# A list-scheduled attention and MLP-mixer kernel on one Trainium2 core: another cost model, order of loads and way of spreading constants

## The chip, the cores and the metric

The kernel runs on one core of one Trainium2 chip. The core has a matrix engine (TensorE, PE in the profile), a vector engine (VectorE, DVE), a scalar engine (ScalarE, ACT), a general engine (GpSimd, POOL), and queues that issue DMAs between the chip's memory and the on-chip buffer SBUF. TensorE writes to PSUM, from which VectorE and ScalarE read. Each engine works through its own instructions in program order and waits at each for the data that it needs.

The metric is the time of one execution on the device in microseconds. The kernel before took 294.46 us, the median of three runs (293.62 to 296.24).

## The reference

Four batches of 768 tokens, 8 heads of 64 (so 512 columns): attention in which each token sees the first 4 tokens and the 128 up to itself, then a residual MLP block with a mixing over tokens and one over channels.

```python
# q, k, v: (4, 8, 768, 64); n_sink = 4, window = 128
scores = q @ k.transpose(0, 1, 3, 2) / sqrt(64)
rel = pos[:, None] - pos[None, :]
keep = (pos[None, :] < n_sink) | ((rel >= 0) & (rel < window))
a = softmax(where(keep, scores, -1e9))
x = (a @ v).transpose(0, 2, 1, 3).reshape(4, 768, 512)

tok = einsum('ts,bsd->btd', w_tok, alpha1 * x + beta1)   # w_tok: 768 x 768
u = x + lam * tok
ch = maximum((alpha2 * u + beta2) @ w_ch1, 0) @ w_ch2    # 512 x 2048, 2048 x 512
out = u + lam * ch
```

All inputs and the output are fp32.

## The kernel before

**The plan.** The body does not issue instructions directly. It adds about a thousand tasks to a `Plan`, each with a priority, the engines that could run it and an estimated cost on each, the tasks it comes after, and the buffers it uses. `Plan.emit` then does list scheduling: it always takes the task that can start earliest by its own clock (ties by priority, then by the earlier end) and emits its instructions on that engine. So the estimated costs, the estimated landing time of a load (`lands`, with all loads on one modelled channel) and the priorities set the order on every engine's queue. The estimates set nothing else: on the chip each instruction waits only for its data and for its buffer. Buffers have a fixed number of homes (`homes`); a task whose buffer kind has no free home is passed over.

**The work.** For batch b:

- `load_qk` (L290) loads 8 pieces of `q` and `k` of 384 KB into `nat` (8 homes); `load_v` (L297) loads 6 pieces of `v` of 256 KB into `vnat` (4 homes). Batch 0's `v` comes as 12 pieces of 128 KB (`load_v0`, L306), six of them in a buffer that occupies one home of `wst`.
- `trans` (L352) casts a `nat` piece to fp16 (`n16`), transposes it on TensorE (`tp`) and copies it to `qkT`. For later batches the cast is GpSimd's and the copy VectorE's.
- `sinks`, `fill_vs`, `scores` and `pv` do the attention: products `S` on TensorE, `E` = exp on ScalarE, the mask on VectorE (for batch 0 the mask is added by TensorE instead), then `pv`, and `x` = `pv` times a reciprocal on VectorE. The scaled `xh` follows, on GpSimd for later batches (`tmp`, then `xh`).
- `tok` (L600) is the mixing over tokens: six accumulating matmuls for each of six token tiles, each needing all six `xh`. The add to `x` follows on VectorE, then the cast `u` on ScalarE.
- `uTs` transposes `u`, and VectorE applies alpha2 and beta2. `mlp1` (`h`, then relu to `hT`) and `mlp2` (`ch`) are the channel MLP; the add of `ch` and the store follow.

On TensorE the attention of batch b+1 is placed between the MLP's matmuls of batch b.

**The weights** are loaded once, in batch 0. `w_tok` comes in 6 pieces, is cast by ScalarE with a running sum (`rs`, the row sums), and is transposed on TensorE to `wtokT`. `w_ch1` and `w_ch2` come in 4 pieces of 1 MB each through `wst` (2 homes); `cast_w1` (L578) makes `w1f`, and `cast_w2` (L586) makes `w2f`, the weights times `lam`. The vectors `lam`, `alpha1` and `beta1` are loaded as broadcasts to all 128 partitions (`load_const`, 256 KB each), and GpSimd makes `la1_b` = alpha1 * lam and `lb1_b` = beta1 * lam.

**The order of loads.** All loads but those of alpha2 and beta2 go through one queue (SP), in the order of the plan. For batch 0: half of `q` and `k`, two `v` pieces, `lam`, `alpha1`, four `v` pieces, the other half of `q` and `k`, six `v` pieces, three of `w_tok`, the first of `w_ch1`, `beta1`, three of `w_tok`, then the other weights. The loads of batch b+1 have priority `w0` (b = 0) or `w0 - 30`, and no predecessor but a free home, so SP also takes them whenever a weight load finds no home.

Of the kernel before, what the change touches and what calls it, by code (L numbers as in the profile page):

```python
# [29 lines left out]
class Task:  # L30
    def __init__(self, prio, engs, fn, after, uses, mode, lands):
        self.prio, self.engs, self.fn, self.uses = prio, engs, fn, uses
        self.mode, self.lands = mode, lands
        self.needs = [a for a in after if a is not None and a.seen is None]
        self.ready = max([0.0] + [a.seen for a in after if a is not None and a.seen is not None])
        self.then = []
        self.seen = None


class Plan:  # L40
# [8 lines left out]
    def add(self, prio, engs, fn, after=(), uses=(), mode=None, lands=0.0):  # L49
        t = Task(prio, engs, fn, after, uses, mode, lands)  # L50
        for b in uses:
            b.left += 1
        for a in t.needs:
            a.then.append(t)
        self.tasks.append(t)
        return t

    def emit(self):
# [13 lines left out]
        channel = 0.0  # L72
        done = 0
        while done < len(self.tasks):
            best = None
            for r, t in open_:
# [57 lines left out]
def kernel(  # L134
# [56 lines left out]
        "wst": (sb, [P, 4, 512], FP32),  # L191
# [5 lines left out]
        "rec": 2, "u16": 4, "uT": 1, "hT": 2, "wst": 2, "d": 4, "S": 2,  # L197
# [14 lines left out]
    alpha2_c = const.tile([P, NC], FP32, name="alpha2_c")  # L212
    beta2_c = const.tile([P, NC], FP32, name="beta2_c")
    rs = const.tile([P, NR], FP32, name="rs")
    nc.scalar.dma_start(alpha2_c, moe_alpha2.rearrange("(c p) -> p c", p=P))
    nc.scalar.dma_start(beta2_c, moe_beta2.rearrange("(c p) -> p c", p=P))
# [6 lines left out]
    )  # L223
    mask0 = const.tile([P, 1, 2 * P], FP16, name="mask0")
# [36 lines left out]
    )  # L261
    bias0 = const.tile([P, 1, 2 * P], FP16, name="bias0")
# [27 lines left out]
    def load_qk(p, b, hp, t):  # L290
# [4 lines left out]
            uses=[bf], lands=1030)  # L295

    def load_v(p, b, r):  # L297
# [4 lines left out]
            uses=[bf], lands=950)  # L302
# [3 lines left out]
    def load_v0(p, G, r):  # L306
        if r == 0:
            v0[G] = Buf(("uT", "wst")[G], [P, NR, 4, D], FP32, f"v0_{G}")
        bf = v0[G]
        done["v0", G, r] = add(  # L310
            p, {SP: 520}, lambda e: nc.sync.dma_start(  # L311
                bf.t[:, r], v[0, 4 * G : 4 * G + 4, r * P : (r + 1) * P, :].rearrange("h p d -> p h d")),
            uses=[bf], lands=470)
# [3 lines left out]
    def load_wtok(p, ti):  # L317
        if ti % 3 == 0:
# [5 lines left out]
            uses=[bf], lands=1000)  # L324
# [3 lines left out]
    def load_w(p, key, src):  # L328
        bf = wst[key] = Buf("wst", None, None, f"wst_{key}")
        done["wst", key] = add(  # L330
            p, {SP: 400}, lambda e: nc.sync.dma_start(bf.t, src), uses=[bf], lands=2600)

    def load_w1(p, i):
        load_w(p, f"w1_{i}", moe_w_ch1[:, i * 512 : (i + 1) * 512].rearrange("(c p) f -> p c f", p=P))

    def load_w2(p, i):
        load_w(p, f"w2_{i}", moe_w_ch2[i * 512 : (i + 1) * 512, :].rearrange("(a p) d -> p a d", p=P))

    def load_const(p, name, tile_, src):
        done[name] = add(  # L340
            p, {SP: 500}, lambda e: nc.sync.dma_start(tile_, src.unsqueeze(0).to_broadcast([P, DM])),
            lands=800)
# [7 lines left out]
    ANY = {DVE: 555, ACT: 835, POOL: 859}  # L350

    def trans(p, b, hp, t, engs, evac, cast_p=None):  # L352
# [20 lines left out]
        a = add(p - 2 if cast_p is None else cast_p, engs, cast, [done["nat", b, hp, t]], [src, n16])  # L373
        a = add(p, {PE: 330}, tr, [a], [n16, pt])
# [5 lines left out]
    def sinks(p, b, Gs=(0, 1)):  # L380
# [24 lines left out]
        a = add(p, {DVE: 360 if n == 1 else 600}, ksf, qk + [done.get(("sk", b - 1, 0))], [o])  # L405
        a = add(p + 0.1, {PE: 240}, mm, [a], [o, pt], mode="col")
        done["sk", b, Gs[0]] = a
        done["es", b, Gs[0]] = add(p + 0.2, {ACT: 595}, ex, [a], [pt, es[b]])

    def fill_vs(p, b):  # L410
        pt = Buf("d", [P, H, D], FP32, f"vsp{b}")

        def mm(e):
            nc.tensor.matmul(pt.t, sel, vf[0][:, :, 0:D], start=True, stop=True)

        def ev(e):
            nc.vector.tensor_mul(vs[:, :, 0:D], pt.t, bmf.to_broadcast([P, H, D]))

        vfs = [done["vf", b, 0]] if b else [done["vf", 0, 0, 0], done["vf", 0, 0, 1]]
        a = add(p, {PE: 215}, mm, vfs, [pt])  # L420
        done["vsmm", b] = a
        prior = [done.get(("pv", b - 1, r, G)) for r in range(NR) for G in range(2)]
        done["vs", b] = add(p + 0.1, {DVE: 690}, ev, [a] + prior, [pt])

    def scores(p, b, j, Gs, bias=False):
# [29 lines left out]
        cost = sum(n * w * 0.42 + (2 * n * w * 0.42 + 100 if bias else 0) for _, _, n, _, _ in units)  # L455
        a = add(p, {PE: cost}, mm, qk, [o] + [u[3] for u in units], mode="row")
        for G, hps, n, pS, eT in units:
# [8 lines left out]
            if not bias:  # L466
# [5 lines left out]
                x_ = add(p + 0.2, {DVE: 60 + 2 * n * w * 0.72}, mk, [x_], [eT])  # L472
# [5 lines left out]
    def pv(p, b, r, G):  # L478
# [25 lines left out]
        if r >= 2:  # L504
            after += [done["vs", b], done["es", b, G if b == 0 else 0]]
            uses.append(es[b])
        a = add(p, {PE: 128 + 250}, mm, after, uses)
# [14 lines left out]
        if b == 0:  # L522
# [6 lines left out]
            done["xh", b, r, G] = add(p + 8.2, {POOL: 730, DVE: 420}, half, [a, done["la1"]], [bx, bh])  # L529
# [20 lines left out]
    def cast_v0(p, G, r):  # L550
        bf = v0[G]
        done["vf", 0, r, G] = add(
            p, {POOL: 400, DVE: 230, ACT: 400},
            lambda e: copy(e, vf[r][:, 4 * G : 4 * G + 4, 0:D], bf.t[:, r]), [done["v0", G, r]], [bf])


    def cast_wtok(p, ti):
# [3 lines left out]

        def cast(e):
            nc.scalar.activation(
                w.t.rearrange("p r i -> p (r i)"), src.t[:, ti % 3, :], AF.Copy,
                accum_out=rs[:, ti : ti + 1])

        def tr(e):
# [6 lines left out]
        done["wtokT", ti] = add(  # L574
            p + 0.2, {DVE: 560, ACT: 810}, lambda e: copy(e, wtokT[:, :, ti * P : (ti + 1) * P], pt.t),
            [a], [pt])

    def cast_w1(p, i):  # L578
        src = wst[f"w1_{i}"]
        for c in range(NC):  # L580
            done["w1", i, c] = add(
                p, {ACT: 600, POOL: 645, DVE: 330},
                lambda e, c=c: copy(e, w1f[:, c, i * 512 : (i + 1) * 512], src.t[:, c, :]),
                [done["wst", f"w1_{i}"]], [src])

    def cast_w2(p, i):  # L586
        src = wst[f"w2_{i}"]
        for a in range(4):
            done["w2", 4 * i + a] = add(
                p, {DVE: 900, POOL: 1400},  # L590
                lambda e, a=a: engine[e].tensor_mul(w2f[:, 4 * i + a, :], src.t[:, a, :], lam_b),  # L591
                [done["wst", f"w2_{i}"], done["lam"]], [src])
# [7 lines left out]
    def tok(p, b, ti):  # L600
# [5 lines left out]
        def mm(e):  # L606
            for si in range(NR):
                nc.tensor.matmul(  # L608
                    pt.t, wtokT[:, si, ti * P : (ti + 1) * P], hs[si].t,
                    start=(si == 0), stop=(si == NR - 1))  # L610
# [10 lines left out]
        def uc(e):  # L621
            copy(e, bu.t, bx.t.rearrange("p h d -> p (h d)"))

        after = [done["wtokT", ti]] + [
            done["xh", b, r, G] for r in range(NR) for G in ((0, 1) if b == 0 else (1,))]
        a = done["tok", b, ti] = add(p, {PE: 6 * 214}, mm, after, [pt] + hs)
        before = [done["xh", b, ti, G] for G in ((0, 1) if b == 0 else (1,))]
        if b == 0:
            before.append(add(p - 0.5, {DVE: 870}, res,
                              before + [done["rs", ti], done["lb1"], done["x", b, ti, 0], done["x", b, ti, 1]],  # L630
                              [bx]))
        a = done["u", b, ti] = add(p + 0.1, {DVE: 690}, ua, [a] + before, [pt, bx])
        done["u16", b, ti] = add(p + 0.2, {ACT: 620}, uc, [a], [bx, bu])

    def uTs(p, b, chk, cp):
# [14 lines left out]
        for ci in range(2):  # L650
            c = 2 * cp + ci

            def ev(e, ci=ci, c=c):
                nc.vector.tensor_scalar(  # L654
                    out=bo.t[:, c, chk * NTOK : (chk + 1) * NTOK], in0=pt.t[:, ci, :],
                    scalar1=alpha2_c[:, c : c + 1], scalar2=beta2_c[:, c : c + 1],
                    op0=ALU.mult, op1=ALU.add)

            done["uT", b, chk, c] = add(p + 0.1 + 0.01 * ci, {DVE: 470}, ev, [a], [pt, bo])
# [62 lines left out]
    for r in range(2):  # L722
        load_v0(at(), 0, r)
    load_const(at(), "lam", lam_b, moe_lam)
    load_const(at(), "a1", la1_b, moe_alpha1)
    for r in range(2, NR):
# [5 lines left out]
    for ti in range(3):  # L732
        load_wtok(at(), ti)
    load_w1(at(), 0)
    load_const(at(), "b1", lb1_b, moe_beta1)
    for ti in range(3, NR):
        load_wtok(at(), ti)
    for i in range(1, 4):
        load_w1(at(), i)
    for i in range(4):  # L740
        load_w2(at(), i)

    done["la1"] = add(-890, {POOL: 1270}, lambda e: nc.gpsimd.tensor_mul(la1_b, la1_b, lam_b),
                      [done["lam"], done["a1"]])
    done["lb1"] = add(-790, {POOL: 1270}, lambda e: nc.gpsimd.tensor_mul(lb1_b, lb1_b, lam_b),
                      [done["lam"], done["b1"]])
    for i, (hp, t) in enumerate(QK_ORDER):
        g = -950 + 5 * i if i < 4 else -890 + 8 * (i - 4)
        trans(g, 0, hp, t, ANY, {DVE: 955, ACT: 880}, cast_p=g - 20)
# [3 lines left out]
    fill_vs(-890, 0)  # L753
# [14 lines left out]
    for b in range(B):  # L768
# [10 lines left out]
        else:  # L779
            seq = [("tok", ti) for ti in range(5)] + [("uT", 0, 0), ("uT", 0, 1), ("tok", 5)]  # L780
# [80 lines left out]
```

## Time and profile before

| | us |
|---|---|
| median of three runs | 294.46 (293.62 to 296.24) |
| the profiled execution | 292.78 |
| its span in the trace | 291.1 |
| TensorE busy in the span | 264.5 |
| VectorE busy | 177.5 |
| ScalarE busy | 116.2 |
| GpSimd busy | 117.6 |
| moved by DMA | 37.01 MB |

The profile is a trace of one execution. A span of 40 slices shows which engine is busy when, a digit for each slice in tenths. Rows of the timeline give start, duration, engine, line and operation, and in brackets how long the engine had been idle before it and who ended that. Rows of a wait give who waited for whom, the total, the number of times and the longest. Names with the number left out stand for all tiles of the name, and `L591` is line 591 of the kernel.

### The profile page before, as it was taken

To read this page: it belongs to the slowest core of one execution; us is meant where nothing else is said; L and a number is where in the kernel's file an instruction comes from. 1 tells how busy PE (TensorE), PEld (TensorE's weight loads), DVE (VectorE), ACT (ScalarE), POOL (GpSimd) and SP (SyncE) were. 2 spreads that over 40 slices of the span, in tenths; PEclk is the share of its full clock that TensorE was granted. 3 is DMA by queue.
4 is the path that set the end of the run, shared out by engine and by line. 5 is a ranking of instruction groups with operands and counts; after the bars stand their busy time and mean duration, and the time that the engine had idled before them with its cause. 6 is when DMAs were issued, how large, how long until landed. Compare 5 with 4: busy or idle time off the path is not lost.

```text
span 291.1 us, 4977 instructions
## 1 busy us (share of the span) xinstructions
PE 264.5 (91%) x1984; PEld 144.8 (50%) x1984; DVE 177.5 (61%) x338; ACT 116.2 (40%) x189; POOL 117.6 (40%) x127
## 2 busy tenths in 40 slices
PE   1789599889594999999999999999999999999994
PEld 0344366555352454565654545665654545665441
DVE  4576998575999744896645417977654336543111
ACT  2489555458361001258772003367741014442000
POOL 4365896361699883340465632202435500000000
PEclk9999789999799899999999999999999999999999
DMA  6999999999970365510021111000001110000111
GB/s 206 295 299 368 386 321 275 373 252 339 309 269 0 108 181 145 155 65 0 2 65 46 72 43 67 0 2 0 3 1 74 72 71 3 0 0 2 72 72 72
DMA packets 43814, 37.01 MB, mean 127 GB/s; under 512 B 27280, under 2 KB 35472, under 8 KB 43792
## 3 DMA queue, kind: packets, MB, share of 16 engines
q1 hardware_dynamic: 42736, 36.71, 40.2%
q8 instruction: 15, 0.25, 0.4%
q10 hardware_dynamic: 1056, 0.00, 0.2%
q14 instruction: 7, 0.06, 0.1%
HBM read 30.41 MB, written 6.29 MB: 126 GB/s over the span
## 4 chain that ended last, share of the span: by engine, by line
PE 66%; DMA 15%; DVE 11%; SPq 4%; issue 1%; POOL 1%; ACT 0%; ACTq 0%; DVEq 0%; POOLq 0%
PE ch L693 27%; PE h L669 25%; DMA wst_w<-in_moe_w_ch_dram 8%; PE tok L608 6%; DMA nat<-in_q_dram 4%; DVE w2f L591 4%; SPq L311 3%; PE pv L493 2%; DVE E L470 2%; PE S L448 2%; DMA beta_c<-in_moe_beta_dram 2%; SPq L294 1%; DMA v<-in_v_dram 1%; PE tp L367 1%; DVE qkT L206 1%; DVE uT L654 1%
## 5 line engine op out<-in xcount | busy, mean ns | idle before, releaser
L669 PE MATMUL h<-uT,w1f 128*128 128x384 f16 x512 | 92.9, 329 | 4.4 <-DVE x L517 3.0
L693 PE MATMUL ch<-w2f,hT 128*128 128x512 f16 x384 | 90.1, 384 | 3.7 <-DVE x L517 3.2
L669 PEld LDWEIGHTS <-w1f 128*128 128x128 f16 x512 | 47.8, 98 | 36.5 <-issue 8.0
L693 PEld LDWEIGHTS <-hT 128*128 128x128 f16 x384 | 36.1, 99 | 45.2 <-DVE x L517 3.7
L675 ACT ACTIVATE hT<-h 128x384 f16<-128x384 f32 x87 | 42.4, 493 | 37.4 <-PE h L669 37.1
L204 ACT CAST u<-x 128x512 f16<-128x512 f32 x24 | 14.9, 619 | 81.7 <-DVE x L619 79.2
L461 ACT ACTIVATE E<-S 128x1024 f16<-128x1024 f32 (+1 forms) x42 | 40.8, 1005 | 5.2 <-PE S L448 4.0
L704 DVE TENSOR_TENSOR x<-x,ch 128x512 f32<-128x512 f32 x24 | 16.5, 688 | 42.9 <-PE ch L693 42.9
L534 POOL TENSOR_TENSOR tmp<-x,la_b 128x512 f32<-128x512 f32 x18 | 24.4, 1356 | 44.8 <-DVE x L517 44.5
L206 POOL CAST n<-nat 128x768 f16<-128x768 f32 x29 | 24.8, 865 | 37.4 <-PE tp L367 27.8
L677 DVE TENSOR_SCALAR hT<-h 128x384 f16<-128x384 f32 x41 | 22.8, 557 | 26.0 <-PE h L669 25.8
L608 PE MATMUL tok<-xh,wtokT 128*128 128x512 f16 x144 | 33.7, 379 | 0.0
L206 DVE COPY qkT<-tp 128x768 f16<-128x768 f16 x28 | 26.6, 951 | 2.4 <-PE tp L367 2.3
L367 PE MATMUL tp<-iden,n 128*128 128x128 f16 x192 | 17.6, 238 | 10.6 <-DVE n L206 5.3
L537 POOL TENSOR_TENSOR xh<-tmp,lb_b 128x512 f16<-128x512 f32 x18 | 24.7, 1374 | 0.9
L470 DVE TENSOR_TENSOR E<-E,maskn 128x1024 f16<-128x1024 f16 x24 | 21.9, 918 | 4.5 <-ACT E L461 4.5
L619 DVE TENSOR_TENSOR x<-x,tok 128x512 f32<-128x512 f32 x24 | 16.4, 685 | 10.8 <-PE tok L608 10.5
L367 PEld LDWEIGHTS <-n 128*128 128x128 f16 x192 | 13.9, 106 | 15.3 <-DVE n L206 5.6
L517 DVE TENSOR_TENSOR x<-pv,rec 128x256 f32<-128x256 f32 x48 | 20.4, 425 | 1.7
L608 PEld LDWEIGHTS <-wtokT 128*128 128x128 f16 x144 | 13.7, 98 | 14.8
L493 PEld LDWEIGHTS <-E 128*128 128x128 f16 x328 | 16.3, 99 | 9.0 <-issue 2.9
L493 PE MATMUL pv<-vf,E 128*128 128x65 f16 x328 | 19.0, 196 | 1.3 <-ACT E L461 1.3
(71 smaller groups left out, 203.5 us busy)
## 6 DMA issues: line engine op xcount, KB each, us to landing
wst_w<-in_moe_w_ch_dram SPq DMA_DIRECT2D x8, 1024.0 KB, 8.4
nat<-in_q_dram SPq DMA_DIRECT2D x16, 384.0 KB, 8.0
nat<-in_k_dram SPq DMA_DIRECT2D x16, 384.0 KB, 7.9
out_dram<-x SPq DMA_DIRECT2D x24, 256.0 KB, 2.0
vnat<-in_v_dram SPq DMA_DIRECT2D x18, 256.0 KB, 4.4
wtn<-in_moe_w_tok_dram SPq DMA_DIRECT2D x6, 384.0 KB, 8.2
v<-in_v_dram SPq DMA_DIRECT2D x12, 128.0 KB, 5.5
lam_b<-in_moe_lam_dram SPq DMA_DIRECT2D x1, 256.0 KB, 5.3
```

The costliest lines, as they stand in the source:

```text
L206: engine[e].tensor_copy(o, i)
L367: nc.tensor.transpose(pt.t[:, r * P : (r + 1) * P], n16.t[:, r, :], iden)
L461: nc.scalar.activation(eT.t, pS.t[:, :, 0 : n * w].rearrange("p e (i w) -> p e i w", i=n), AF.Exp, scale=scale)
L470: nc.vector.tensor_mul(ev, ev, m.to_broadcast(list(ev.shape)))
L493: nc.tensor.matmul(po.t[:, hl, :], eT.t[:, e_, off + i, c : c + P], vf[j][:, h, :], start=(r < 2 and n == 0), stop=(n == len(parts) - 1 an ...
L534: nc.gpsimd.tensor_mul(tmp.t, bx.t.rearrange("p h d -> p (h d)"), la1_b)
L537: nc.gpsimd.tensor_add(bh.t, tmp.t, lb1_b)
L608: nc.tensor.matmul(pt.t, wtokT[:, si, ti * P : (ti + 1) * P], hs[si].t, start=(si == 0), stop=(si == NR - 1))
L669: nc.tensor.matmul(ph.t, w1f[:, c, fi * P : (fi + 1) * P], bu.t[:, c, chk * NTOK : (chk + 1) * NTOK], start=(c == 0), stop=(c == NC - 1))
L675: nc.scalar.activation(bh.t[:, fi, :], ph.t, AF.Relu)
L677: nc.vector.tensor_scalar_max(bh.t[:, fi, :], ph.t, 0.0)
L693: nc.tensor.matmul(pc.t, bh.t[:, fi, nt * P : (nt + 1) * P], w2f[:, fi, :], start=(fi == 0), stop=(fi == NF - 1))
```

## The change

The scheduler gets a resource that VectorE and GpSimd share. Every task can be marked `port`; in the plan, a GpSimd task and a marked VectorE task do not overlap.

```diff
-    def add(self, prio, engs, fn, after=(), uses=(), mode=None, lands=0.0):
+    def add(self, prio, engs, fn, after=(), uses=(), mode=None, lands=0.0, port=False):
...
                 for e in t.engs:
-                    key = (max(free[e], at), r, free[e] + t.engs[e])
+                    at_e = max(free[e], at)
+                    if e == POOL or (e == DVE and t.port):
+                        at_e = max(at_e, port)
+                    key = (at_e, r, at_e + t.engs[e])
...
             free[e] = start + cost
+            if e == POOL or (e == DVE and t.port):
+                port = free[e]
             t.at = (e, start, free[e])
             if e == SP:
-                channel = max(channel, free[e] + 1500.0) + t.lands
+                channel = max(channel, free[e] + 1600.0) + t.lands
```

Marked are the casts (`trans`, `cast_v0`, `cast_wtok`, `cast_w1`), the `w2f` products, the masks, batch 0's `xh`, its residual term and the small copies of `sinks`. Many estimates change, for example a `w2f` product from 900 (VectorE) and 1400 (GpSimd) to 700 and 1270, and the landing times of loads by some 5 to 25%.

The staging of `w_ch1` and `w_ch2` is halved in size and doubled in number, and so are their loads:

```diff
-        "wst": (sb, [P, 4, 512], FP32),
+        "wst": (sb, [P, 2, 512], FP32),
...
-        "rec": 2, "u16": 4, "uT": 1, "hT": 2, "wst": 2, "d": 4, "S": 2,
+        "rec": 2, "u16": 4, "uT": 1, "hT": 2, "wst": 4, "d": 4, "S": 2,
...
     def load_w1(p, i):
-        load_w(p, f"w1_{i}", moe_w_ch1[:, i * 512 : (i + 1) * 512].rearrange("(c p) f -> p c f", p=P))
+        for c in range(0, NC, 2):
+            load_w(p + 0.1 * c, f"w1_{i}_{c}",
+                   moe_w_ch1[c * P : (c + 2) * P, i * 512 : (i + 1) * 512].rearrange("(c p) f -> p c f", p=P))
```

`load_w2` is split the same way. The second half of batch 0's `v` now takes two homes of `wst`, three pieces in each.

The constants come as rows of 2 KB on ScalarE's queue. VectorE multiplies them on one partition, and TensorE spreads each with a product of a column of ones in fp32; alpha2 and beta2 are loaded as 8 rows and transposed by TensorE. `load_const` and the two GpSimd products go.

```diff
+    rows = [sb.tile([1, DM], FP32, tag=f"x_{6 + i}", bufs=1, name=f"row{i}") for i in range(3)]
+    for o_, i_ in zip(rows, (moe_lam, moe_alpha1, moe_beta1)):
+        nc.scalar.dma_start(o_, i_.unsqueeze(0))
+    nc.scalar.dma_start(ab_row[0:NC], moe_alpha2.rearrange("(c p) -> c p", p=P))
+    nc.scalar.dma_start(ab_row[NC : 2 * NC], moe_beta2.rearrange("(c p) -> c p", p=P))
...
+    def spread(p, name, src, o):
+
+        pt = Buf("d", None, None, f"b_{name}")
+        a = add(p, {PE: 900}, lambda e: nc.tensor.matmul(pt.t, ones_r, src, start=True, stop=True),
+                [done.get(name)], [pt])
+        done[name] = add(p + 0.1, {DVE: 600, ACT: 600}, lambda e: copy(e, o, pt.t), [a], [pt])
...
+    def spread_rows():
+        done["la1"] = add(-985, {DVE: 640}, lambda e: nc.vector.tensor_mul(rows[1], rows[1], rows[0]), port=True)
+        done["lb1"] = add(-984, {DVE: 640}, lambda e: nc.vector.tensor_mul(rows[2], rows[2], rows[0]), port=True)
+        for p_, n_, i_, o_ in ((-934, "la1", 1, la1_b), (-800, "lam", 0, lam_b), (-799, "lb1", 2, lb1_b)):
+            spread(p_, n_, rows[i_], o_)
+        pt = Buf("d", [P, 2 * NC], FP32, "abT")
+        a = add(-850, {PE: 200}, lambda e: nc.tensor.transpose(pt.t, ab_row, iden8), [], [pt])
+        done["ab2"] = add(-800, {DVE: 100, ACT: 230}, lambda e: copy(e, ab2, pt.t), [a], [pt])
```

The row sums of `w_tok` come from TensorE, six one-column matmuls for each tile, and any of three engines may cast `w_tok`:

```diff
+        def row(e):
+            for si in range(NR):
+                nc.tensor.matmul(
+                    pr.t, wtokT[:, si, ti * P : (ti + 1) * P], ones_c,
+                    start=(si == 0), stop=(si == NR - 1))
...
-        a = add(p, {ACT: 1030}, cast, [done["wtn", ti]], [src, w])
-        done["rs", ti] = a
+        a = add(p, ANY, lambda e: copy(e, w.t.rearrange("p r i -> p (r i)"), src.t[:, ti % 3, :]),
+                [done["wtn", ti]], [src, w], port=True)
```

The loads have another order and other predecessors. The weights follow batch 0's inputs; batch 1's `q` and `k` come after `w_ch1` by priority, then `w_ch2`, then batch 1's `v`. The loads of batches 2 and 3 come after the `ch` product of token tile 3 in the batch two before, and the transposes of a next batch after `tok` 2:

```diff
         if b == 0:
...
+            for i, (hp, t) in enumerate(QK_ORDER):
+                load_qk(t0 + 100 + i, 1, hp, t)
             for i in range(4):
-                cast_w2(w0 + 26 + 4 * i, i)
+                load_w2(t0 + 200 + i, i)
+                cast_w2(w0 + 22 + 4 * i, i)
+            for r in range(NR):
+                load_v(t0 + 300 + r, 1, r)
+        if 0 < b < B - 1:
+            late = done["ch", b - 1, 3]
+            for i, (hp, t) in enumerate(QK_ORDER):
+                load_qk(w0 - 20 + i, b + 1, hp, t, late)
+            for r in range(NR):
+                load_v(w0 - 10 + r, b + 1, r, late)
...
-            pl = w0 - (0 if b == 0 else 30)
-            for i, (hp, t) in enumerate(QK_ORDER):
-                load_qk(pl + 0.5 * i, nb, hp, t)
-            for r in range(NR):
-                load_v(pl + 4 + 0.5 * r, nb, r)
...
-                    trans(p, nb, hp, t, {POOL: 859}, {DVE: 955})
+                    trans(p, nb, hp, t, {POOL: 829}, {DVE: 955, ACT: 800}, wait=done["tok", b, 2])
```

In batch 0, `tok` 0 and 1 are split into a task of four matmuls and one of two. Some tasks get a second engine: the `u` cast also GpSimd, the evictions of `uT` and of later batches' `qkT` also ScalarE. The sums of the first keys (`fill_vs`) of batch 0 are split by half of the heads, and batch 0's score products and sink exponentials rank ahead of all else:

```diff
-        a = done["tok", b, ti] = add(p, {PE: 6 * 214}, mm, after, [pt] + hs)
+        a = None
+        for sis in ((0, 1, 2, 3), (4, 5)) if b == 0 and ti < 2 else (range(NR),):
+            after = [done["wtokT", ti], a] + [
+                done["xh", b, r, G] for r in sis for G in ((0, 1) if b == 0 else (1,))]
+            a = add(p, {PE: 215 * len(sis)}, mm(sis), after, [pt] + [hs[si] for si in sis])
+        done["tok", b, ti] = a
...
-        done["u16", b, ti] = add(p + 0.2, {ACT: 620}, uc, [a], [bx, bu])
+        done["u16", b, ti] = add(p + 0.2, {ACT: 620, POOL: 640}, uc, [a], [bx, bu])
...
+        if bias:
+            p = p - 1000
         a = add(p, {PE: cost}, mm, qk, [o] + [u[3] for u in units], mode="row")
...
-            seq = [("tok", ti) for ti in range(5)] + [("uT", 0, 0), ("uT", 0, 1), ("tok", 5)]
+            seq = [("tok", ti) for ti in range(4)]
+            seq += [("uT", 0, 0), ("tok", 4), ("uT", 0, 1), ("tok", 5)]
```

More of the change, by code (lines that the diff above doesn't have):

```diff
@@ L349, with trans @@
     xh = {}
-    ANY = {DVE: 555, ACT: 835, POOL: 859}
-    def trans(p, b, hp, t, engs, evac, cast_p=None):
+    ANY = {DVE: 560, ACT: 831, POOL: 829}
+    def trans(p, b, hp, t, engs, evac, cast_p=None, wait=None):
         if b not in qkT:
@@ L586, in cast_w2 @@
     def cast_w2(p, i):
[L587 to L592, printed above, removed]
+        for a in range(4 * i, 4 * i + 4):
+            src = wst[f"w2_{a - a % 2}"]
+            done["w2", a] = add(
+                p, {DVE: 700, POOL: 1270},
+                lambda e, a=a, src=src: engine[e].tensor_mul(w2f[:, a, :], src.t[:, a % 2, :], lam_b),
+                [done["wst", f"w2_{a - a % 2}"], done["lam"]], [src], port=True)
```

182 lines of the change are left out of this document (96 added, 86 removed).

## The prediction

> **What bounds the kernel now.** I read the slices of the page first, then the windows by batch, then what TensorE waited for, then the DMA issues of the stretch where it waits.
>
> ```profile
> span 291.1 us, 4977 instructions
> ...
> PE   1789599889594999999999999999999999999994
> ...
> DMA  6999999999970365510021111000001110000111
> ```
>
> A slice is 7.3 us. From slice 16 on TensorE is full. Its gaps lie in the first 110 us, and there the DMA engines are full until slice 12.
>
> ```profile
> 39.10:111.85 72.75, 63.88 (x469) 34.42 (x467) 54.52 (x85) 28.49 (x49) 50.01 (x47) 0.95 0.79 235
> 111.85:173.77 61.92, 61.64 (x483) 34.42 (x481) 38.01 (x75) 25.57 (x41) 25.89 (x26) 1.00 0.19 61
> 173.77:235.69 61.92, 61.64 (x482) 34.47 (x481) 37.99 (x75) 25.57 (x41) 19.04 (x16) 1.00 0.07 27
> 235.69:291.10 55.41, 51.59 (x288) 26.98 (x286) 20.40 (x36) 11.96 (x23) 0.00 (x0) 1.00 0.10 38
> ```
>
> Columns: stretch, length, busy time of TensorE, its weight loads, VectorE, ScalarE and GpSimd, granted clock, DMA share, GB/s. Each stretch starts with the first `tok` matmul of a batch. Batches 1 and 2 take 61.92 us with 61.64 busy, so they are TensorE's own work; the last has no next batch to prepare. Batch 0 takes 72.75 us for the same work, 10.8 us more, and 39.1 us pass before it. What TensorE waited for in batch 0:
>
> ```profile
> PE ch L693 <- DVE x L517: 3.2, 1, 3.2
> PE h L669 <- DVE x L517: 3.0, 1, 3.0
> PE uTp L646 <- ACT hT L675: 1.1, 1, 1.1
> PE h L669 <- DVE hT L677: 0.9, 1, 0.9
> PE ch L693 <- POOL w2f L591: 0.5, 1, 0.5
> ```
>
> That is 8.7 us; the rest of the 10.8 is matmuls slowed after the two long gaps. VectorE is late at both because `w2f` products stand in its queue, and these are late and long:
>
> ```profile
> L591 DVE TENSOR_TENSOR w2f<-wst_w,lam_b x8: 694/1747/1759, 71.5 to 91.2; 128x512 f16<-128x512 f32 x8
> L591 POOL TENSOR_TENSOR w2f<-wst_w,lam_b x8: 1707/1714/1771, 71.6 to 90.7; 128x512 f16<-128x512 f32 x8
> ...
> L743 POOL TENSOR_TENSOR la_b<-la_b,lam_b x1: 1267/1267/1267, 11.2 to 11.2; 128x512 f32<-128x512 f32 x1
> ```
>
> They are late because of what is loaded before them. Between 40 and 82 us:
>
> ```profile
> DMA packets 16487, 13.00 MB, mean 310 GB/s; under 512 B 10673, under 2 KB 13751, under 8 KB 16482
> ...
> wst_w<-in_moe_w_ch_dram SPq DMA_DIRECT2D x5, 1024.0 KB, 8.3
> nat<-in_q_dram SPq DMA_DIRECT2D x6, 384.0 KB, 8.6
> nat<-in_k_dram SPq DMA_DIRECT2D x6, 384.0 KB, 8.6
> vnat<-in_v_dram SPq DMA_DIRECT2D x8, 256.0 KB, 9.1
> ```
>
> ```profile
> 32.66 0.37 SPq L294 DMA_DIRECT2D nat<-in_k_dram  x1
> ```
>
> Batch 0 and batch 1 need 16 `nat` loads, and the sixteenth was issued at 32.7 us. So the 12 here are batches 2 and 3: 12 x 0.393 MB = 4.72 MB, at 310 GB/s 15.2 us of a full stream ahead of weights that batch 0 waits for.
>
> **The change, part by part.** Sums are against the profiled execution: 292.78 us, 1.7 more than its span, and 1.7 less than the median of 294.46.
>
> *Weights of batch 0.* The loads of batches 2 and 3 are now planned after the `ch` of token tile 3 of the batch two before. The 15.2 us of stream go from before the last `w2` piece; so do the three broadcast constants (3 x 256 KB = 0.79 MB, 2.5 us). The last `wst` issue stands at 82.4 (row below), so the last piece would land some 17 us earlier, about 70 instead of 88.
>
> ```profile
> L331 SPq DMA_DIRECT2D wst_w<-in_moe_w_ch_dram x8: 367/496/3229, 19.6 to 82.4; - x8
> ```
>
> The staging buffers are halves now: 16 issues of 512 KB in place of 8. [...] Queue order: with both free slots taken by `w1_0`, SP still sends `q`, `k` and four `v` loads of batch 1 before `w1_1`, as before. TensorE reaches the second product (`ch`) of batch 0 at about 34 + 9 (`tok`, `uT`) + 21 (`h`) + 7 of the next batch's attention = 71 us, just after the pieces land. So I do not take all 10.8 us away: with the products still to be made (16 pieces, 0.69 us alone on VectorE, 1.27 on GpSimd) 3 us stay. Gain 7.8; bounds 3 (only the `w2f` and `h` waits shorten) and 10.8.
>
> *The port model, new costs.* No work goes; the order does. In the plan a GpSimd task and a VectorE task marked `port` exclude each other; the chip goes on overlapping them. Alone 0.69 + 1.27 = 1.96 us for a pair; together the rows show 1.75 and 1.71, ending together. The Trainium skill (SBUF — State Buffer, Who interferes with whom) says that a VectorE instruction with two SBUF inputs contends with a GpSimd one that reads SBUF, through an exclusive lock for the whole instruction. By that, eight pairs would take 15.7 us, by the rows 14.0; the rows agree that they contend and disagree on the size by a tenth. What the plan can gain is in the 7.8 already; what it can lose is a rival below. `u16` may go to GpSimd, `uT` and the `qkT` copies to ScalarE: relief for VectorE, which is 54.5 of 72.75 us busy in batch 0. Zero by itself, since TensorE is the bound behind it.
>
> *The first attention stage.* Rows of before:
>
> ```profile
> 5.01 0.34 SPq L341 DMA_DIRECT2D lam_b<-in_moe_lam_dram  x1
> 5.32 0.82 PE L367 MATMUL tp<-iden,n 128*128 128x128 f16 x6 [5.32 <-DVE n L206]
> 5.39 0.44 SPq L341 DMA_DIRECT2D la_b<-in_moe_alpha_dram  x1
> ...
> 9.82 1.06 PE L443 MATMUL S<-bias,iden 128*128 128x512 f16 x2
> ...
> 10.81 0.66 PE L448 MATMUL S<-qkT 64*128 64x256 f16 x4
> ...
> 11.73 0.41 ACT L204 CAST vf<-v 128x256 f16<-128x256 f32 x1 [1.72 <-DMA v<-in_v_dram]
> ...
> 13.23 1.93 ACT L461 ACTIVATE E<-S 128x1024 f16<-128x1024 f32 x2
> ```
>
> ```profile
> 31.86 1.88 DVE L614 SCALAR_TENSOR_TENSOR x<-lb_b,rs,x 128x512 f32<-128x512 f32 x2
> ...
> 34.68 0.82 PE L367 MATMUL tp<-iden,n 128*128 128x128 f16 x6 [3.07 <-POOL n L206]
> ...
> 39.10 1.46 PE L608 MATMUL tok<-xh,wtokT 128*128 128x512 f16 x6
> ```
>
> Gone: (a) the gap before 34.68, 3.1 us: a transpose of batch 1, whose load was issued at 22.28, stood ahead of batch 0's last `pv`. `trans` now waits in the plan for `tok` 2. Late next are the last `pv`'s `x` and `xh` on VectorE, behind residual terms such as that at 31.86, so I take 3.0 of it. (b) `lam_b` and `la_b` ahead of the second half of `q` and `k`: 0.52 MB at 289 GB/s, 1.8 us. (c) `tok` 0 and 1 in two parts: four of six matmuls, two thirds of 1.46 us, run before the last `xh`: 2 x 0.97 us; I take 1.0, as little else is ready then.
>
> ```profile
> 10.00:20.00 10.00, 8.07 (x76) 3.38 (x74) 7.13 (x15) 6.75 (x11) 5.46 (x7) 1.00 1.18 289
> ```
>
> Added: (d) in the plan the row loads on ScalarE's queue cost no time, so the row products lead VectorE's queue and the transpose of `ab_row` and three `spread` matmuls lead TensorE's. On the chip these wait for five small loads issued from 0.8 us on; the like ones of before landed 4.2 and 5.2 us after issue.
>
> ```profile
> alpha_c<-in_moe_alpha_dram ACTq DMA_DIRECT2D x1, 2.0 KB, 4.2
> beta_c<-in_moe_beta_dram ACTq DMA_DIRECT2D x1, 2.0 KB, 5.2
> ```
>
> Behind them wait all `tp`, and behind VectorE's two products the first cast. A 512-column f16 matmul at that time takes 0.53 us (1.06 for two). The trace has no f32 matmul: from f16 speed (3 x 0.53 = 1.6) to twice, for twice the bytes (3.2); I take 2.4. The first `tp` then comes at about 5 to 6.5 + 2.4, 8 to 9 instead of 5.3. Cover: `E` started at 13.23 though its scores were there at 11.5, because ScalarE stood behind a `v` cast that waited for its load; this hides 1.8 of some 3. Cost 1.2; bounds 0 and 4. The Trainium skill (FP8 and Floating Point Precision, TensorE Precision Notes) gives true FP32 four passes; by that the three are an estimated 6.4 us and the total 4 us more. No run here shows it. (e) 36 one-column `row` matmuls: like six transposes, 0.34 us a set (row below), 2.0 us on TensorE, mostly before `xh` is there; 0.5. Without that cover 2.0. The accumulator reads on ScalarE (6 x 0.2) and the two GpSimd products (2 x 1.3) go, three evictions and six small copies come: even.
>
> ```profile
> 115.31 0.34 PE tp L367 x6
> ```
>
> ```profile
> L563 ACT ACTIVATION_READ_ACCUMULATOR wt<-wtn 128x1 f32 x5 | 1.1, 212 | 0.0
> ```
>
> Net 3.0 + 1.8 + 1.0 - 1.2 - 0.5 = 4.1; bounds 0 and 7.
>
> *Batches 1 to 3.* Only 0.28 us of gap each, so nothing to win. The loads of a next batch start later (rival 3); the reordered `uT` can leave a gap of some tenths each. Cost 0.3; bounds -0.5 and 4.
>
> Sum: 292.78 - 7.8 - 4.1 + 0.3 = 281.0; moved up by the 1.7 to the median's level, 282.7. I say **282.5 us**.
>
> **The rivals.**
> 1. *The stream is earlier, VectorE stays late* (0.18). `w2f`, `xh` and the masks still collide, since the chip does not know the plan: VectorE's 54.5 and GpSimd's 50.0 us are both in batch 0. Against it: up to 8 of VectorE's (8 x (1.75 - 0.69)) are the `w2f` products' lengthening, which comes of their bunching after 71 us. Then 3 instead of 7.8 is won: 287.5.
> 2. *It does not do what it says* (0.11): first-come greedy order still fills the queue with `q`, `k`, `v` of batch 1 whenever a staging slot is taken, halves turn round too slowly, and (d) takes (a) to (c): 1 to 3 us won, 292.5. For it: batch 1's loads precede `w1_1` in both. Against it: batches 2 and 3 cannot.
> 3. *Slower* (0.08): loads of batches 2 and 3 no longer run ahead. They sit in SP's queue behind output stores, which wait for VectorE (before: up to 34 us), and the `tp` of the next batch stand in TensorE's order. Place: the starts of batches 1 and 2. Today scores of the next batch begin 20 us into the stretch, which 3.15 MB of `q` and `k` at 310 GB/s (10 us) fit into. Each us that the loads come later than their planned place stops TensorE. From 6 us in both batches on, the 12 won are spent; with 8 in both, 298.
>
> ```profile
> SPq L707 <- DVE x L704: 87.9, 16, 34.4
> ...
> 131.82 0.33 PE sk L397 x4
> ```
>
> **How the numbers follow.** Forecast 0.63, own range 277 to 287; rivals 0.18, 0.11, 0.08. The range 275 to 292 takes in the forecast with its bounds, rival 1 and half of rival 2. About 1% (2.9 us) is what a measurement of this kernel can tell from no change. Below 291.5: forecast and rival 1, 0.81. Within: rival 2, 0.11. Above 297.4: rival 3, 0.08.
>
> **What would show it.** The first `tok` near 35 instead of 39.1; no gap before a `tp` of batch 1; the three `spread` matmuls before the first `tp`. No `nat` issue of batch 2 before the last `wst`, which lands near 70; `w2f` done by about 73; batch 0's stretch near 65; batches 1 and 2 at 62. Wrong, if the stretch of batch 0 stays above 70, the first `tok` is not earlier, or batches 1 and 2 pass 64.

## The result and the profile after

The changed kernel takes 278.65 us (median of 4 runs, 277.85 to 279.44) against 294.19 before (a fourth run joins the three above): a ratio of 0.946, with a 95% interval of 0.9405 to 0.9515. A run that took over 1.5% more than the fastest of its kernel counts as slow, and ratios leave it out. The profiled execution took 279.44 us with a span of 277.6, so 13.3 us less than the profiled one of before. On record were 282.5 us, with a range of 275 to 292.

The page of the changed kernel, the same rows as before:

```profile
span 277.6 us, 5062 instructions
...
PE   0999999999899999999999999999999999999994
...
DMA  7999999888001699100000799000011110000121
```

A slice is 6.9 us here. After the first slice the DMA engines are busy at 70% and more to about 69 us, where before they were to about 87; then they rest and come back around 90 us: that is batch 2's input, which used to run ahead of the weights. TensorE has no hole left after the first slice. Its busy time is the same as before, 264.8 us against 264.5; what fell is its idle time, from 26.6 to 12.8 us.

The windows from one batch's first `tok` to the next (length, busy time of TensorE, weight loads, VectorE, ScalarE, GpSimd, granted clock, DMA share, GB/s):

```profile
35.96:99.52 63.56, 61.70 (x499) 34.72 (x497) 51.01 (x89) 34.42 (x59) 38.38 (x37) 1.00 0.62 188
99.52:160.89 61.37, 61.37 (x482) 34.34 (x481) 33.93 (x71) 29.48 (x45) 26.40 (x28) 1.00 0.34 99
160.89:222.26 61.37, 61.37 (x482) 34.34 (x481) 34.39 (x72) 29.33 (x45) 24.03 (x24) 1.00 0.27 80
222.26:277.60 55.34, 51.66 (x289) 27.08 (x287) 11.39 (x19) 20.05 (x39) 1.23 (x2) 0.99 0.10 38
```

So the first `tok` comes 3.1 us earlier, batch 0's stretch is 9.0 us shorter (72.59 to 63.56), and batches 1 and 2 win 0.55 us each. Together that is 13.3 of the 13.5 us by which the span fell; the last stretch gives the rest. (The windows of before in the prediction are cut 0.16 us behind the first `tok` of batch 1, which starts at 111.69; measured from there, the stretch is 72.59 and not 72.75.) All that TensorE still waits for in the whole run:

```profile
PE abT L792 <- DMA ab_row<-in_moe_beta_dram: 6.9, 1, 6.9
PE pv L523 <- DVE E L500: 1.2, 2, 1.0
PE pv L523 <- DVE vs L446: 0.6, 1, 0.6
PE pv L516 <- DVE x L547: 0.3, 1, 0.3
```

The two long waits for VectorE's `x` (3.2 and 3.0 us) are gone. The weights' pieces and the products made of them, by tile:

```profile
L358 SPq DMA_DIRECT2D wst_w<-in_moe_w_ch_dram x16: 367/368/2549, 20.1 to 64.6; - x16
L636 DVE TENSOR_TENSOR w2f<-wst_w,lam_b x13: 679/685/1759, 59.7 to 75.7; 128x512 f16<-128x512 f32 x13
...
L636 POOL TENSOR_TENSOR w2f<-wst_w,lam_b x3: 1274/1493/1717, 56.1 to 66.6; 128x512 f16<-128x512 f32 x3
```

The last load is issued at 64.6 instead of 82.4. And 13 of 16 products are now VectorE's, at a median of 0.685 us. Before it was 8 and 8, at 1.75 and 1.71. At TensorE's front the products that spread the constants cost more than the prediction allowed for:

```profile
6.89 0.24 PE L792 MATMUL abT<-iden,ab_row 8*128 8x8 f32 x1 [6.89 <-DMA ab_row<-in_moe_beta_dram]
7.00 2.04 PE L618 MATMUL b_lam<-row,ones_r 1*128 1x512 f32 x2
8.84 1.91 PE L618 MATMUL b_la<-row,ones_r 1*128 1x512 f32 x2
10.55 1.91 PE L618 MATMUL b_lb<-row,ones_r 1*128 1x512 f32 x2
12.39 2.74 PE L393 MATMUL tp<-iden,n 128*128 128x128 f16 x24
```

The first `tp` starts at 12.39 instead of 5.32.

### The profile page after: what moved, and what is told of

It is laid out like the page before. It is cut to its first block, busy times and chain, and to the rows that moved or that the text cites. A ratio compares the mean times of both kernels' runs of the same rounds, so it can differ in the third digit from the quotient of the medians.

```text
span 277.6 us, 5062 instructions
## 1 busy us (share of the span) xinstructions
PE 264.8 (95%) x2028; PEld 145.6 (52%) x2028; DVE 155.9 (56%) x317; ACT 134.8 (49%) x219; POOL 108.2 (39%) x127
## 4 chain that ended last, share of the span: by engine, by line
PE 85%; DVE 8%; DMA 3%; ACT 1%; issue 1%; ACTq 0%; SPq 0%; DVEq 0%
PE ch L746 30%; PE h L722 26%; PE tok L654 11%; PE tp L393 4%; PE pv L523 3%; PE S L476 3%; PE uTp L696 2%; DMA wst_w<-in_moe_w_ch_dram 2%; DVE E L500 2%; DMA ab_row<-in_moe_beta_dram 2%; DVE x L547 1%; PE S L471 1%; PE pv L516 1%; DVE w2f L636 1%; DVE xh L556 1%; PE b_lam L618 1%
## 5 line engine op out<-in xcount | busy, mean ns | idle before, releaser
L722 PE MATMUL h<-uT,w1f 128*128 128x384 f16 x512 | 91.6, 326 | 0.1
L746 PE MATMUL ch<-w2f,hT 128*128 128x512 f16 x384 | 87.8, 379 | 0.0
L728 ACT ACTIVATE hT<-h 128x384 f16<-128x384 f32 x91 | 44.4, 494 | 20.7 <-PE h L722 20.1
L565 POOL TENSOR_TENSOR tmp<-x,la_b 128x512 f32<-128x512 f32 x18 | 24.7, 1371 | 64.3 <-DVE x L547 64.3
L211 ACT CAST u<-x 128x512 f16<-128x512 f32 x20 | 12.4, 619 | 61.3 <-DVE x L666 61.3
L213 POOL CAST n<-nat 128x768 f16<-128x768 f32 x27 | 23.7, 896 | 21.4 <-PE tp L393 10.6
L730 DVE TENSOR_SCALAR hT<-h 128x384 f16<-128x384 f32 x37 | 20.6, 557 | 17.9 <-PE h L722 17.1
L666 DVE TENSOR_TENSOR x<-x,tok 128x512 f32<-128x512 f32 x24 | 16.4, 686 | 12.9 <-PE tok L654 12.8
L523 PEld LDWEIGHTS <-E 128*128 128x128 f16 x328 | 15.6, 98 | 8.2 <-issue 1.8
L500 DVE TENSOR_TENSOR E<-E,maskn 128x1024 f16<-128x1024 f16 x24 | 19.4, 837 | 0.0
L211 ACT COPY qkT<-tp 128x768 f16<-128x768 f16 x19 | 15.1, 801 | 3.4 <-PE tp L393 3.3
L393 PE MATMUL tp<-iden,n 128*128 128x128 f16 x192 | 16.1, 231 | 0.0
```

The lines of the kernel that those rows point to most:

```text
L211: nc.scalar.copy(o, i)
L213: engine[e].tensor_copy(o, i)
L393: nc.tensor.transpose(pt.t[:, r * P : (r + 1) * P], n16.t[:, r, :], iden)
L500: nc.vector.tensor_mul(ev, ev, m.to_broadcast(list(ev.shape)))
L523: nc.tensor.matmul(po.t[:, hl, :], eT.t[:, e_, off + i, c : c + P], vf[j][:, h, :], start=(r < 2 and n == 0), stop=(n == len(parts) - 1 an ...
L565: nc.gpsimd.tensor_mul(tmp.t, bx.t.rearrange("p h d -> p (h d)"), la1_b)
```

## The experiments

Each run is timed against the kernel before on the same chip; ratios are to that. In three groups of runs the kernel before took 293.0, 293.3 and 293.3 us.

### The changed kernel once more

> The changed kernel once more, for comparison on the same chip: 278.65 us within 1 us by every theory.

278.90 us, ratio 0.952 (0.948 to 0.956). Its first `tok` starts at 35.07 where the first profile has 35.96: so much do two profiles of one kernel differ there. Batch 0's stretch is 63.58.

### The load order, added to the kernel before and taken from the changed one

```diff
+            late = done.get(("ch", b - 1, 3))
...
-                load_qk(pl + 0.5 * i, nb, hp, t)
+                load_qk(pl + 0.5 * i, nb, hp, t, late)
...
-                load_v(pl + 4 + 0.5 * r, nb, r)
+                load_v(pl + 4 + 0.5 * r, nb, r, late)
```

> The kernel before with one part of the change: the loads of batches 2 and 3 are planned after the ch product of token tile 3 of the batch two before. If the loads ahead of the weights made batch 0 late (15.2 us of stream), its stretch of 72.75 us falls to 65 to 67 and the time by 6 to 8 us, to about 287. If VectorE and GpSimd stay late whatever the loads do, because the plan does not know that they share a port, the stretch falls by less than 3 us and the time stays above 291.

288.6 us, ratio 0.986 (0.983 to 0.990): 4.4 us won, between the two theories. Batch 0's stretch fell to 68.4, not to 66. The last load of a weight is issued at 66.9, nearly as early as in the changed kernel (64.6), but the products are still shared between both engines. By tile:

```profile
L591 POOL TENSOR_TENSOR w2f<-wst_w,lam_b x10: 1264/1712/1772, 59.3 to 77.9; 128x512 f16<-128x512 f32 x10
L591 DVE TENSOR_TENSOR w2f<-wst_w,lam_b x6: 682/911/1746, 59.2 to 80.1; 128x512 f16<-128x512 f32 x6
```

and TensorE keeps a wait of the old kind:

```profile
PE ch L693 <- DVE x L517: 2.4, 1, 2.4
```

So early weights alone do not end the waiting. The reverse, in the changed kernel:

```diff
-            late = done["ch", b - 1, 3]
+            late = None
...
-                load_qk(w0 - 20 + i, b + 1, hp, t, late)
+                load_qk(w0 - 30 + 0.5 * i, b + 1, hp, t, late)
```

(and `load_v` likewise, at `w0 - 26 + 0.5 * r`).

> The changed kernel with the loads of batches 2 and 3 free to go early, as before. If the load order carries batch 0's gain, its stretch of 63.56 us grows by 4 to 8 us and the time is 283 to 287. If the other edits have made the weights independent of it, less than 1 us.

285.38 us, ratio 0.973 (0.969 to 0.976): 6.5 us lost against the 278.90 of the same chip. Only 2.9 of it lies in batch 0; 3.7 lie in batch 1. The windows of both:

```profile
35.88:102.34 66.46, 63.12 (x503) 35.28 (x501) 55.96 (x92) 31.74 (x55) 38.70 (x41) 1.00 0.84 259
102.34:167.39 65.05, 62.29 (x476) 34.29 (x476) 34.58 (x74) 29.41 (x45) 29.65 (x30) 0.97 0.21 62
```

The chain before batch 1 says why (start, length, what):

```profile
90.47 0.70 DVE x L757
91.19 0.36 SPq L760
91.64 3.02 DMA vnat<-in_v_dram
94.67 1.65 POOL tmp L565
96.32 0.56 POOL vf L213
96.87 1.22 POOL xh L568
```

A `v` load sits in SP's queue behind an output store, GpSimd's scaling of batch 1's `x` starts as that load lands, and `tok` waits 2.5 us for `xh`. By the order of issues this load is the twelfth of `vnat`, so it is batch 2's last. Batch 2's casts of `v` now stand in GpSimd's queue between the scalings of batch 1, and the one before waits 8.3 us for TensorE's `pv`:

```profile
92.91 1.06 POOL L213 CAST vf<-vnat 128x512 f16<-128x512 f32 x1 [8.26 <-PE pv L523]
```

In the changed kernel GpSimd has no such cast between 69 and 98 us. So batch 1 loses time because work of batch 2 was taken ahead of it, on SP's queue and on GpSimd's; the share of each was not measured. An input load behind an output store is the mechanism of the prediction's slower rival, but it appears when the loads are free to run ahead, not when they are held back.

### The shared port in the plan

```diff
             if e == POOL or (e == DVE and t.port):
-                port = free[e]
+                port = 0.0
```

> The changed kernel without the shared port in the plan (all other costs and orders of it stay). If the port model only reorders work that hides behind TensorE, within 2 us of 278.65. If the port model carries the gain, the gaps of batch 0 come back and the time is 284 or more.

281.87 us, ratio 0.963 (0.960 to 0.967), against 0.946 and 0.952 of the changed kernel: 3 us are lost, between the two expectations. The first `tok` is not later (35.23); batch 0's stretch is 67.92, 4.4 us longer. By tile:

```profile
L636 POOL TENSOR_TENSOR w2f<-wst_w,lam_b x8: 1264/1455/1787, 58.2 to 73.8; 128x512 f16<-128x512 f32 x8
L636 DVE TENSOR_TENSOR w2f<-wst_w,lam_b x8: 678/1131/1758, 61.0 to 75.5; 128x512 f16<-128x512 f32 x8
```

The products are eight and eight again, and their medians are 1.46 and 1.13 us. What this does can be read from the chain in that stretch, which is VectorE's queue from 62 to 78 us, products and masks by turns:

```profile
63.46 0.69 DVE w2f L636
64.15 0.47 DVE hT L730
64.62 0.60 DVE E L500
65.22 1.67 DVE w2f L636
66.89 1.68 DVE E L500
```

The two of 1.67 and 1.68 stand beside the plain 0.69 and 0.60: they overlap products of GpSimd (64.56 to 66.35 and 66.62 to 68.03). Without the port in its plan the scheduler takes GpSimd for a product because it is idle, and pays on VectorE for it. TensorE then waits 1.7 us for VectorE's `vs` and 1.7 us for its `x`; in the changed kernel the longest such wait is 0.6.

```diff
+                    if e == POOL or (e == DVE and t.port):
+                        at_e = max(at_e, port)
```

This in the kernel before, with its loads held back, its `port` marks as in the change and its old costs:

> The kernel before with loads of batches 2 and 3 held back and with the shared port in the plan, at its old costs. Held-back loads alone gave 288.6. If the port model is worth the 3 us that its removal cost in the changed kernel, 285 to 286.5. If it needs the new costs, 288 or more.

287.0 us, ratio 0.977 (0.972 to 0.982), against 0.986 without the port. By the medians 1.6 us are won, by the ratios 2.8, by the profiled spans 0.4 (286.8 to 286.4). So the port model helps in the old kernel too, by an amount that these runs do not fix, and it does not give the rest of the gain. The products do run apart there (medians 0.69 us on VectorE and 1.27 on GpSimd), but batch 0's stretch is not shorter: the first `tok` comes at 36.18 instead of 38.99, the stretch is 73.28 instead of 68.40, and batch 1's is 59.52 instead of 61.92. In batch 0's stretch TensorE now waits most for evictions of its results by VectorE and ScalarE:

```profile
PE h L676 <- DVE qkT L213: 1.9, 1, 1.9
PE h L676 <- ACT hT L682: 1.6, 1, 1.6
...
PE tp L374 <- DVE uT L661: 1.4, 1, 1.4
```

### The transposes' wait for `tok` 2

```diff
-        a = add(p, {PE: 330}, tr, [a], [n16, pt])
+        a = add(p, {PE: 330}, tr, [a, wait], [n16, pt])
...
-                    trans(p, nb, hp, t, {POOL: 859}, {DVE: 955})
+                    trans(p, nb, hp, t, {POOL: 859}, {DVE: 955}, wait=done["tok", b, 2])
```

> The kernel before with one part of the change: the transposes of a next batch come after tok 2 in the plan. If the 3.1 us gap ahead of batch 0's last pv was on the path, the first tok comes about 3 us earlier, at 36, and the time falls by 1 to 3 us (batch 0 still waits for its weights, which gives part of it back). If the last xh were late anyway, less than 1 us.

293.17 us, ratio 1.000 (0.998 to 1.003). The first `tok` did come earlier, at 35.53, by 3.6 us, but batch 0's stretch grew by 3.1, to 75.65, and batches 1 and 2 by 0.35 each. After five `tok` matmuls TensorE waits for GpSimd's last `xh`, as the second case of the expectation has it, and later there is a wait of 3.1 us for VectorE's `vs`:

```profile
PE pv L493 <- DVE vs L417: 3.1, 1, 3.1
PE tok L608 <- POOL xh L526: 2.3, 1, 2.3
```

With the loads held back as well:

> The kernel before with both: loads of batches 2 and 3 held back, transposes of a next batch after tok 2. By the theory that load order and this wait are the change's gain, 9 to 11 us: about 284. By the theory that the costs and the port model carry it, 3 us or less: about 291.

290.01 us, ratio 0.989 (0.986 to 0.993), no better than the loads alone. And in the changed kernel without it (`wait` left out of the `trans` call):

> The changed kernel without the wait of a next batch's transposes for tok 2 in the plan. If that wait is what keeps them behind batch 0's last pv, a gap of 2 to 4 us before a tp comes back and the first tok is that much later: 280 to 282. If the new costs and landing times keep them in place anyway, less than 1 us.

278.76 us, ratio 0.950 (0.947 to 0.953): nothing, against 278.90. The waits of TensorE are the same four as in the changed kernel. The gap at 34.7 does not come back, so in the changed kernel it is not this line that keeps the transposes in place. The other edits do it without it; which of them, no run shows.

### The spread products at TensorE's front

```diff
-    spread_rows()
     for i, (hp, t) in enumerate(QK_ORDER):
...
+    spread_rows(done["qkT", 0, 0, 1], done["qkT", 0, 1, 1])
```

(the row products come after the first of these two tasks, the spread products and the `ab` transpose after the second).

> The changed kernel with the row products planned after the second and the spread products and the ab transpose after the fourth qkT copy of batch 0. In the changed kernel TensorE has nearly no gap from 7 us on, and the first tp waits for 5.4 us of spread products and, before them, for the rows. If that front is on the path, the first tp is back near 5.3 us, the first tok comes 3 to 5 us earlier (31 to 33) and the time is 274 to 276. If the loads, ScalarE's exponentials or VectorE set the end of the first stage anyway, less than 1 us: 278.

279.11 us, ratio 0.950 (0.946 to 0.955): nothing. The first `tp` is at 4.52, 7.9 us earlier, and yet the first `tok` is at 37.40; batch 0's stretch, at 61.82, then makes up for it. The wait of 6.9 us for the rows has turned into as long a wait for VectorE's casts, ahead of the first four transposes:

```profile
PE tp L393 <- DVE n L213: 6.9, 4, 4.5
```

In the timeline the second score product of batch 0 still runs at the early slow rate, then comes a spread product, also slow, and two more scores, slow too; the other two spread products, from 31 us on, take 1.1 us each:

```profile
12.14 1.03 PE L471 MATMUL S<-biasn,iden 128*128 128x512 f16 x2
13.11 0.61 PE L476 MATMUL S<-qkT 64*128 64x256 f16 x4
13.65 2.07 PE L618 MATMUL b_la<-row,ones_r 1*128 1x512 f32 x2
15.65 1.03 PE L471 MATMUL S<-biasn,iden 128*128 128x512 f16 x2
...
31.12 1.12 PE L618 MATMUL b_lam<-row,ones_r 1*128 1x512 f32 x2
```

Next, the products in f16 in place of f32, at the front and late:

```diff
+    rows16 = [sb.tile([1, DM], FP16, tag=f"x_{9 + i}", bufs=1, name=f"row16_{i}") for i in range(3)]
...
-    ones_r = const.tile([1, P], FP32, name="ones_r")
+    ones_r = const.tile([1, P], FP16, name="ones_r")
...
-            spread(p_, n_, rows[i_], o_)
+            spread(p_, n_, rows16[i_], o_)
```

> The changed kernel with the three spread products in f16 instead of f32, at the same place at TensorE's front (the rows are rounded to f16 before they are spread). They took 1.71 to 1.91 us each. If the f32 form costs several passes, they take about 0.45 each, the first tp comes 4 us earlier, and if TensorE's work is the bound from 7 us on, the time falls by 2 to 4 us, to 275 to 277. If other engines or loads set the end of the first stage, less than 1 us.

279.58 us, ratio 0.949 (0.944 to 0.954): nothing. The three products shrank as expected, from 1.7 to 1.9 us each to 0.44, in the chain:

```profile
6.87 0.24 PE abT L794
7.11 0.44 PE b_lam L619
7.55 0.44 PE b_la L619
```

and the first `tp` comes at 9.83, but the first `tok` stays at 35.73. The 2.6 us by which the first `tp` is earlier turn into waits of TensorE, for VectorE's casts and for `wtokT`:

```profile
PE tp L394 <- DVE n L213: 1.4, 1, 1.4
PE rs L602 <- ACT wtokT L211: 0.9, 1, 0.9
```

In this profile the granted clock is also low right behind them, 0.60 from 35.73 to 40 us, and the first `tok` matmuls run slowly. The two of the six runs with a mean granted clock of 1.00 took 276.80 and 277.30 us, so a small gain that the clock takes back is not excluded.

> The changed kernel with the f16 spread products (rows rounded to f16) planned after the fourth qkT copy, as in the late variant. That variant saved nothing although its first tp came 7.9 us earlier; its three products still took 4.3 us of TensorE, one of them and the first scores at the early slow rate. If TensorE's own work is the bound, 3 us less of it gives 275 to 276.5. If the loads or the exponentials hold the first stage, within 1 us of 279.

277.55 us, ratio 0.945 (0.939 to 0.950), and the runs spread from 275.75 to 283.61 (the other five to 279.83), so against the changed kernel (0.946 and 0.952) this is unclear. In the profile (span 274.8) the first `tok` is at 31.82, some 3.7 us earlier than in the changed kernel, and batch 0's stretch is 64.89, 1.3 longer. Up to the first `tok` TensorE is idle for 7.1 us here and busy for 24.7; in the changed kernel it is idle for 7.3 and busy for 28.7. So what is shorter is TensorE's own work, not its waits. It is the best median of all that ran, but a gain over the change is not shown.

### The size of the staging buffers

```diff
-        "wst": (sb, [P, 2, 512], FP32),
+        "wst": (sb, [P, 4, 512], FP32),
...
-            load_w(p + 0.1 * c, f"w1_{i}_{c}",
+        load_w(p, f"w1_{i}", moe_w_ch1[:, i * 512 : (i + 1) * 512].rearrange("(c p) f -> p c f", p=P))
```

> The changed kernel with weights staged in two buffers of 1 MB pieces as before, in place of four of 512 KB. If the finer staging keeps the stream of weights moving, batch 0 loses 2 to 4 us: 281 to 283. If the weights are early enough in either, less than 1 us.

279.29 us, ratio 0.951 (0.946 to 0.956), span 277.3: nothing. Halves and wholes land early enough alike.

## Why the prediction was right

It was right in size and in place: 11.8 us of gain were forecast for the profiled execution, 13.3 came, and the first `tok` (near 35), batch 0's stretch (near 65), the last weight (near 70) and the `w2f` products (done by about 73) were measured at 35.96, 63.56, 64.6 + 4.7 and 76.4. The late products cost nothing, since the first `ch` started at 76.2 and not at the 71 of the prediction. That the total is near is in part luck: the load order was given what the port model and other edits brought, and a front that was priced too low cost nothing more.

**The weights of batch 0** (forecast 7.8, measured 9.0). The load order is the largest single part: without it the changed kernel loses 6.5 us, of which 2.9 lie in batch 0. But the prediction worked out all of its 7.8 from earlier weights. In the kernel before it gave 4.4, and there VectorE stayed late with the weights early, just as rival 1 said.

**The port model** was priced at nothing beside the 7.8; it is worth about 3 us (4.4 in batch 0's stretch). The prediction compared 1.96 us for a pair in turn with 1.75 for a pair together and saw no loss in overlapping. That sum leaves out what matters: in turn, VectorE is held for 0.69 us and then free for masks and evictions that TensorE waits for; together, it is held for 1.75. With the port in the plan, most products are not paired at all, 13 of 16 on VectorE. The Trainium skill (SBUF — State Buffer, Who interferes with whom) says that the shared port pair is an exclusive lock. The rows agree that one engine's work is paid for by the other, and remain a tenth below the sum of the two (1.75 against 1.96).

**The transposes' wait (a)**, 3.0 us, named the right gap, but `wait` is not worth it: alone in the kernel before it moves the first `tok` by 3.6 us and the time by nothing, since the last `xh` and VectorE's `vs` are late there, and without it the changed kernel is the same. In the changed kernel the gap is gone for another reason, and the first stage won 3.1 us where 4.1 were forecast.

**The front (d)** was mis-sized: the three products took 5.4 us (7.0 to 12.4) instead of 2.4, and the first `tp` started at 12.39, not at 8 to 9. Part of the reason is known: the f32 form costs 1.71 us (8.84 to 10.55) where f16 costs 0.44 at the same early rate, a factor of 3.9. The Trainium skill (FP8 and Floating Point Precision, TensorE Precision Notes) gives four passes for true FP32; the runs agree. By that sentence's sum the total would have been 4 us more, and it is not. Moving the products away, or making them four times shorter, shows no gain either: TensorE then waits for VectorE's casts (6.9 us in the late f32 variant). So the cover was larger than the 1.8 us that the prediction gave it.

**Staging halves, row sums, constants, split `tok`**: the halves measure nothing (279.29). The row sums (e, a cost of 0.5), the broadcasts ahead of `q` and `k` (b, a gain of 1.8) and the split (c, a gain of 1.0) were not tried by themselves.

**Batches 1 to 3**: 0.3 us of cost were forecast, 1.1 were won (0.55 twice). The held-back loads did not arrive late: TensorE waits for nothing after batch 0.

**What stays open.** Load order (6.5) and port (3), if their losses add up, leave some 5 of the 14.4 us between 293.3 and 278.9. Trials of the new costs, of the second engines for `u`, `uT` and `qkT`, and of the split `tok` by themselves were not made. That the kernel before with both edits still waits for evictions (`qkT`, `hT`, `uT`) speaks for the second engines; it is argued, not shown. Nor is it settled what would shorten the first stage. In the changed kernel TensorE is busy for all but 0.4 us from 6.89 to 35.96, so its own work ends that stage; the late f16 variant, with 4 us less of such work, ends it at 31.8, but a shorter total is not shown.

## What to carry to other kernels

When the DMA stream is full, list what lies in it ahead of the thing that the critical engine waits for, and count the bytes that nobody needs yet: here the loads of later batches cost 4.4 us in one kernel and 6.5 in the other. Telling a scheduler of a resource that two engines share can pay even if the total throughput is no better in turn than together (about 3 us here), because the engine that others wait for is then free sooner. And a gap that is removed at one place must be followed to the end of the run: the first `tok` came 3.6 us earlier with one line, and all of it was given back.

## What the hardware showed beside

The early slow rate of TensorE lasts for very different times. The windows show a granted clock of 1.00 there, but the traces' records of the clock begin only at 17.36 us in the changed kernel, 11.94 in the late f16 variant, 15.59 in the early one and 18.67 in the late f32 variant, and the windows count the time before as 1.00. Two 512-column f16 products take 0.93 to 1.06 us then, by the rows, and 0.61 later. In the changed kernel TensorE is busy without a break from 6.89 us on, and still slow at 16.67:

```profile
16.67 0.93 PE L471 MATMUL S<-biasn,iden 128*128 128x512 f16 x2
...
18.18 0.61 PE L471 MATMUL S<-biasn,iden 128*128 128x512 f16 x2
```

In the late f16 variant, with the first `tp` at 4.55 and gaps behind it, it is fast from 12.03 on:

```profile
8.34 1.60 PE L394 MATMUL tp<-iden,n 128*128 128x128 f16 x12 [0.97 <-DVE n L213]
...
10.52 1.06 PE L472 MATMUL S<-bias,iden 128*128 128x512 f16 x2
...
12.03 0.61 PE L472 MATMUL S<-biasn,iden 128*128 128x512 f16 x2
```

The Trainium skill (TensorE: Matmul & The Clock Gate, What's actually happening) puts the change at about 3.4 us of sustained activity. The late f16 variant agrees (3.6 us from the `tp` at 8.34 to 11.94); the changed kernel does not (10.5 us from 6.89 to 17.36). It would, nearly, if products of a single row, which fill 7.0 to 12.4 us there, did not count as activity. But the late f32 variant is still slow at 12.14, before its first such product at 13.65 and after the same kinds of products from 8.43 on, with gaps of 0.22 us at most. So this alone does not explain it, and no run tested it by itself.
